# Re-ordering VectorE's and TensorE's lists in the first attention of a fused attention and GELU MLP

## The chip, the cores and the metric

The kernel runs on one core of one Trainium2 chip. Times are device microseconds (us) of one execution. Engines go by the names of the profile: PE is TensorE (PEld its weight loads), DVE is VectorE, ACT is ScalarE, POOL is GpSimd, and SP is the sync engine, which here only issues DMAs.

## The reference

Inputs are q, k and v of shape (8 batches, 12 heads, 448 positions, 64 wide), two gain rows g_q and g_k, and two weight matrices, 768 x 2048 and 2048 x 768. Attention runs on RMS-normed q and k; its output, with the heads side by side, goes through a two-layer MLP with the tanh form of GELU.

```python
q_n, k_n = (rmsnorm(q, g_q), rmsnorm(k, g_k))
scores = scale * np.matmul(q_n, k_n.transpose(0, 1, 3, 2))
attn = np.exp(scores - max);  attn = attn / (sum(attn) + 1e-09)
attn_out = np.matmul(attn, v)            # -> x, (3584, 768), heads side by side
h = x @ w_in
out = (0.5 * h * (1.0 + np.tanh(c * (h + 0.044715 * h * h * h)))) @ w_out
```

## The kernel before, in words

**Units.** A batch is cut into three chunks c = 0, 1, 2 of four heads. The 448 positions are cut into seven key tiles t = 0 to 6 of 64 positions. A *unit* (c, t) is four concurrent 64x64 matmuls (line 335) that make the scores of one key tile for four heads, 128 x 896 numbers, and one ACT exp of them (`ex`, line 339). A batch has 21 units; u0 to u20 below are those of batch 0, so u7 is the first of the middle chunk and u14 the first of the last chunk. The scores go to two PSUM buffers in turn (three from batch 1 on), so a unit's matmuls wait for the exp of the unit two before.

**What a chunk needs before its units.** Raw q and k arrive by DMA. Squares (line 161 on ACT, 163 on POOL) are summed on DVE (`total`, line 172). The inverse root of the mean comes from a log and an exp on ACT (`rsqrt`) in batch 0. For batch 1 DVE works it out with Newton steps: `rsqrt_newton` (lines 226 to 241) for chunks 0 and 2 and `rsqrt_last` (lines 253 to 263) for chunk 1. `normed` (line 275) multiplies; on DVE it reads the root from PSUM, on POOL from SBUF. `turn` (line 293) transposes the seven 128x128 pieces of a normed q or k on PE into a PSUM tile `tp`, and `put` (k: line 302, q: line 304 on ACT or 306 on DVE) copies that into `qT` or `kT`, k with the gains. Pieces 0 to 3 are called `t_first`, pieces 4 to 6 `t_rest`; `normed`, `turn` and `put` take either alone. A unit (c, t) needs all of its chunk's qT, but only piece t of kT.

**What comes after a chunk's units.** `products(..., 0)` sums the exps over the keys with matmuls against `ones` (line 386), `products(..., 1)` multiplies them with v. `turned` (395) transposes the sums on DVE, `recips` takes reciprocals of one column (401) and spreads them back with a second transpose of 128 x 896 (402), and `quad_x` (415) multiplies and writes xT, the MLP's input.

**PSUM.** The tag `mm` of the pool `ps_m` has two buffers that are handed out in turn. In batch 0 the takers are, in program order, the `tp` tiles, the tile `root` (inverse roots of chunk 2), and pairs of `os` tiles (`spared`, line 366), which hold the key sums of chunks 1 and 2. Each new taker waits until the tile two before it in that order has been read for the last time. `oall` holds the products, and also the roots of some chunks and the target `o` of `idle`.

**The order of the work.** It is written out by hand: each engine runs its list in program order. `first_attention` (582) loops over the 21 units of batch 0 and runs the entries of `mid` (lines 730 to 765) with the same number behind each. A slot below is such a number. Behind u20 come the remaining products, the last `quad_x`, and the first MLP layer of batch 0: `mm1_pair` (matmuls at 475, GELU at 480) and `mm1` (424, 430). In the loop over f, `m1` (784 to 792) places batch 1's sums, roots, norms and turns between these: `trans(1, c)` turns and puts q and k of a chunk; chunk 2 goes through DMA transposes instead (316). Then `attention(1, ...)` begins, with groups of units between the second layer's matmuls (445).

**At the start.** Sixteen `idle` matmuls (line 268) of a zero tile keep PE active while the first q and k arrive; pairs of them are placed in slots 0 to 4 and 9. DVE makes the zero tile with four memsets (81), and `ones` and `rows` with one each (634, 635).

Of the kernel before, what the change touches and what calls it, by code (L numbers as in the profile page):

```python
# [17 lines left out]
def kernel(  # L18
# [11 lines left out]
    nc = tc.nc  # L30
# [188 lines left out]
    def rsqrt_newton(b):  # L219


        rinvs[b] = smp.tile([P, NCH, 2, 2, NT], F32, tag="rinv", name="rinv")
        cs, flat = slice(0, NCH - 1), "p c n a t -> p (c n a t)"
        y, ms = rinvs[b][:, cs].rearrange(flat), sss[b][:, cs].rearrange(flat)
        t = smp.tile([P, NCH * 4 * NT], F32, tag="lg", name="lg")[:, :(NCH - 1) * 4 * NT]
        nc.vector.tensor_scalar(ms, ms, 1.0 / D, 1e-6, op0=ALU.mult, op1=ALU.add)
        nc.vector.tensor_scalar(
            y.bitcast(I32), ms.bitcast(I32), -0.5, float(0x5F3759DF), op0=ALU.mult, op1=ALU.add
        )
        for i in range(3):  # L230
            nc.vector.tensor_mul(t, y, y)
            nc.vector.scalar_tensor_tensor(t, t, -0.5, ms, op0=ALU.mult, op1=ALU.mult)
            if i < 2:
                nc.vector.scalar_tensor_tensor(y, t, 1.5, y, op0=ALU.add, op1=ALU.mult)
        m = 4 * NT
        for c in (1, 0):
            dst = y[:, c * m:(c + 1) * m] if c else place(b, c)
            nc.vector.scalar_tensor_tensor(  # L238
                dst, t[:, c * m:(c + 1) * m], 1.5, y[:, c * m:(c + 1) * m],
                op0=ALU.add, op1=ALU.mult,  # L240
            )

    def rsqrt_last(b):
# [44 lines left out]
    def turn(b, c, n, ts=slice(0, NT)):  # L288

        if ts.start == 0 and ts.stop == NT:  # L290
            tps[n] = ps_m.tile([128, 1024], BF16, tag="mm", name="tp")
        for t in range(ts.start, ts.stop):
            nc.tensor.transpose(  # L293
                tps[n][:, t * 128:(t + 1) * 128],
                nrms[n, b, c][:, t].rearrange("p a d -> p (a d)"), ident,
            )

    def put(b, c, n, ts=slice(0, NT), eng=nc.vector):
        dst = (kT if n == "k" else qT_of(b))[:, c, ts]
        src = tps[n][:, :TR].rearrange("p (t r s) -> p t r s", r=2, s=R)[:, ts]  # L300
        if n == "k":
            nc.vector.tensor_scalar(dst, src, gcol[:, 0:1], None, op0=ALU.mult)  # L302
        elif eng is nc.scalar:
            nc.scalar.copy(dst, src)
        else:
            nc.vector.tensor_copy(dst, src)
# [85 lines left out]
    def turned():  # L392
        st = oas["st"] = stp.tile([128, 2, S // 32, 32], F32, tag="st", name="st")
        for r in range(2):
            nc.vector.transpose(st[:, r].rearrange("p a b -> p (a b)"), oas[0][r])  # L395

    def recips():

        rb = oas["rb"] = stp.tile([128, 2, S], F32, tag="rb", name="rb")
        rc = smp.tile([128, 2 * S // 32], F32, tag="rc", name="rc")  # L400
        nc.vector.reciprocal(rc, oas["st"].rearrange("p r a b -> p (r a) b")[:, :, 0])
        nc.vector.transpose(  # L402
            rb.rearrange("p r s -> p (r s)"), rc.to_broadcast([128, 2 * S // 32, 32])
        )

    def quad_x(b, c):
        if c == 0:
# [251 lines left out]
    def warm():  # L659
        return oall[0][:, :S]  # L660
# [59 lines left out]
    for a in range(2):  # L720
# [5 lines left out]
    def turn_rest():  # L726
        tps["k"] = ps_m.tile([128, 1024], BF16, tag="mm", name="tp")
        turn(0, 0, "k", t_rest)

    mid = [(0, lambda: idle(2, warm())),  # L730
           (1, turn_rest, lambda: idle(2, warm())),
           (2, lambda: rsqrt(0, 1, near=(0, 1)), lambda: idle(2, warm())),
           (3, lambda: put(0, 0, "k", t_rest), lambda: normed(0, 1, "q", nc.vector),
            lambda: normed(0, 1, "k", nc.vector, t_first),
            lambda: normed(0, 1, "k", nc.vector, t_rest), lambda: idle(2, warm())),
           (4, lambda: idle(2, warm())),
           (5, lambda: turn(0, 1, "q"), lambda: put(0, 1, "q")),
           (6, lambda: turn(0, 1, "k"), lambda: put(0, 1, "k", t_first),
            lambda: put(0, 1, "k", t_rest)),
           (7, lambda: total(0, 2, "q"), lambda: total(0, 2, "k"),  # L740
            lambda: products(0, 0, 0, 0, 3)),
           (8, lambda: products(0, 0, 0, 3), lambda: turned(),
            lambda: rsqrt(0, 2, near=(1,)), lambda: normed(0, 2, "q", nc.gpsimd),
            lambda: normed(0, 2, "k", nc.vector, t_first),
            lambda: normed(0, 2, "k", nc.vector, t_rest), lambda: recips(),
            lambda: square(1, 0, "q", nc.gpsimd), lambda: w_in_part(1, 2),
            lambda: square(1, 0, "k", nc.gpsimd),
            lambda: w_out_part(0), lambda: load_v(1, 0, HP),
            lambda: square(1, 2, "q", nc.gpsimd), lambda: square(1, 2, "k", nc.gpsimd),
            lambda: w_out_part(1)),  # L750
           (9, lambda: idle(2, warm())),
           (10, lambda: products(0, 0, 1, 0, 3)),
           (11, lambda: products(0, 0, 1, 3)),
           (12, lambda: turn(0, 2, "q"), lambda: put(0, 2, "q"), lambda: turn(0, 2, "k"),
            lambda: put(0, 2, "k", t_first), lambda: put(0, 2, "k", t_rest),
            lambda: quad_x(0, 0)),

           (14, lambda: spared(), lambda: products(0, 1, 0, 0, 4)),
           (15, lambda: products(0, 1, 0, 4), lambda: turned(), lambda: recips()),
# [15 lines left out]
    def normed_both(b, c, eng):  # L775
        for n in "qk":
            normed(b, c, n, eng)

    m2 = []
    for b in range(B):  # L780
        m1, side, behind, ends = [], [], [], []
        if b == 0:

            m1 = [(0, lambda: total(1, 0, "k"),
                   lambda: total(1, 2, "q"), lambda: total(1, 2, "k"),
                   lambda: rsqrt_newton(1), lambda: normed_both(1, 2, nc.gpsimd)),
                  (2, lambda: total(1, 1, "q"), lambda: total(1, 1, "k"),
                   lambda: normed_both(1, 0, nc.vector), lambda: rsqrt_last(1),
                   lambda: normed_both(1, 1, nc.vector)),
                  (4, lambda: transposed(1, 2)),  # L790
                  (5, lambda: trans(1, 0)),
                  (7, lambda: trans(1, 1))]
            side += [(1, lambda: late_loads(2, 0)), (4, lambda: gain(1, 2)),
                     (2, lambda: late_loads(2, 1), lambda: late_loads(2, 2))]

            for n in "qk":
                sqs[n, 2, 1] = [
                    nrmp.tile([P, NT, 2, D], BF16, tag=f"nrm{m}", name="sq")
                    .rearrange("p t a d -> p (t a d)").bitcast(F32)
                    .rearrange("p (a t d) -> p a t d", a=1, t=NT) for m in "qk"  # L800
                ]
            for c, slots in ((0, (4, 4)), (1, (4, 4))):
                for n, slot in zip("qk", slots):
                    for hs in (slice(0, 1), slice(1, 2)) if c else (both,):
                        side.append(
                            (2, lambda c=c, n=n, hs=hs: square(2, c, n, nc.gpsimd, hs)))
                        behind.append((slot, lambda c=c, n=n, hs=hs: total(2, c, n, hs)))
        elif b + 1 < B:

            m1.append((0, lambda: gpsimd_waits(ess[b, NCH - 1][:1, 0, :1])))  # L810
            for c in range(NCH):
                if b == 1 and c + 1 == NCH:
                    m1 += [(0, lambda: total(2, 2, "q")), (0, lambda: total(2, 2, "k")),
                           (0, lambda: rsqrt_last(2))]
                m1 += [(0, lambda c=c: normed_both(b + 1, c, nc.gpsimd)),
                       (4 * c + 4, lambda c=c: transposed(b + 1, c))]
            m1 += [(9, lambda: gain(b + 1, 0)), (14, lambda: gain(b + 1, 1))]
# [73 lines left out]
```

## Time and profile before

| what | value |
|---|---|
| median of three runs | 405.93 us (405.3 to 406.69) |
| the profiled execution, its own time | 405.01 us |
| its span, first to last instruction | 403.2 us |
| granted TensorE clock | 1.000 |
| busy: PE / ACT / DVE / POOL | 393.8 / 280.1 / 259.8 / 121.3 us |
| PE busy from 52 us to 403 us (351 us) | 347.51 us |
| PE busy from 8 us to 30 us (22 us) | 19.07 us |
| first exp of batch 0 begins | 9.06 us |
| last exp of batch 0 ends | 29.65 us |
| first MLP matmul (line 475) begins | 30.41 us |
| first matmul of the second layer (line 445) begins | 51.70 us |

A busy time is a union over the engine's instructions; matmul ends are modelled, so a short wait of PE can be hidden in it. A timeline row gives start, length, engine, line, operation, tiles, shapes and count, and in brackets the idle time before it with what ended it. Neighbouring instructions on DVE and ACT overlap by some 0.08 to 0.1 us in the rows, so the distance from one start to the next is a little shorter than the length. The profiled execution took 0.92 us less than the median; the span is 1.8 us shorter than that execution's own time.

### The profile page before, as it was taken

What the parts mean: (1) busy time and instruction counts of PE and PEld (TensorE: products, weight loads), DVE (VectorE), ACT (ScalarE), POOL (GpSimd) and SP (SyncE); (2) the same over time, 40 slices, a digit from 0 to 9 for tenths busy, and PEclk for the clock granted to TensorE, in tenths of its full rate; (3) what the DMA queues carried; (4) which work ended last, traced back from release to release, by engine and by line L of the source; (5) the groups of instructions that cost most, each with busy time, mean ns of one, the idle gap of its engine ahead of it and who ended that gap; (6) DMA issues with size and microseconds to landing.
All of it is one profiled execution on the core that took longest, in us unless ns stands there. A gap on an engine that the chain in (4) does not pass through costs nothing.

```text
span 403.2 us, 8092 instructions
## 1 busy us (share of the span) xinstructions
PE 393.8 (98%) x3321; PEld 209.8 (52%) x3321; DVE 259.8 (64%) x438; ACT 280.1 (69%) x381; POOL 121.3 (30%) x101
## 2 busy tenths in 40 slices
PE   7899999999999999999999999999999999999996
PEld 3365555555555555554555555555555545555564
DVE  5989968975796369845699357963698405990010
ACT  6995398768974887847975789748878359744301
POOL 5992307454007230183004540072301800000000
PEclk9999999999999999999999999999999999999999
DMA  8999995898515954169612948149513511210033
GB/s 293 318 214 207 196 225 187 236 232 230 96 39 115 245 101 140 41 170 280 109 41 63 253 64 220 40 86 265 78 41 80 115 24 39 50 46 23 2 78 80
DMA packets 65561, 54.07 MB, mean 134 GB/s; under 512 B 37364, under 2 KB 60532, under 8 KB 65524
## 3 DMA queue, kind: packets, MB, share of 16 engines
q1 hardware_dynamic: 53184, 41.48, 39.0%
q0 software_dynamic: 12112, 11.80, 19.0%
q8 instruction: 26, 0.43, 0.4%
q10 hardware_dynamic: 228, 0.28, 0.2%
q14 instruction: 11, 0.09, 0.1%
HBM read 45.61 MB, written 11.01 MB: 140 GB/s over the span
## 4 chain that ended last, share of the span: by engine, by line
PE 89%; DVE 5%; ACT 2%; DMA 1%; issue 1%; POOL 0%; DVEq 0%
PE o L445 38%; PE h L424 24%; PE t L335 9%; PE t L386 8%; PE t L475 8%; ACT ex L339 2%; DVE ss L172 2%; PE o L386 1%; PE tp L293 1%; DMA rawq<-in_q_dram 1%; DVE nrmq L275 1%; DVE nrmk L275 0%; DVE st L395 0%; DVE xT L415 0%; DVE rb L402 0%
## 5 line engine op out<-in xcount | busy, mean ns | idle before, releaser
L339 ACT ACTIVATE ex<-t,shift 128x896 bf16<-128x896 f32 x168 | 157.6, 1005 | 22.7 <-PE t L335 20.1
L445 PE MATMUL o<-wout,g 128*128 128x384 bf16 (+1 forms) x912 | 156.8, 324 | 0.0
L445 PEld LDWEIGHTS <-g 128*128 128x128 bf16 x912 | 83.6, 98 | 67.8 <-issue 18.8
L424 PE MATMUL h<-xT,win 128*128 128x448 bf16 x516 | 99.1, 352 | 0.0
L172 DVE TENSOR_REDUCE ss<-sq 128x14 f32<-128x896 f32 (+3 forms) x45 | 44.3, 999 | 48.8 <-ACT sq L161 45.8
L424 PEld LDWEIGHTS <-win 128*128 128x128 bf16 x516 | 50.5, 98 | 47.1
L430 ACT ACTIVATE g<-h 128x448 bf16<-128x448 f32 x86 | 46.6, 543 | 28.2 <-PE h L424 23.1
L455 DVE COPY osb<-o 128x384 f32<-128x384 f32 x41 | 22.7, 554 | 52.4 <-PE o L445 50.7
L475 PE MATMUL t<-xT,win 128*128 128x448 bf16 x252 | 49.6, 352 | 0.0
L335 PE MATMUL t<-qT,kT 64*64 64x448 bf16 x672 | 47.1, 359 | 2.1 <-DVE kT L302 1.0
L480 ACT ACTIVATE g<-t 128x896 bf16<-128x896 f32 x21 | 18.4, 915 | 33.8 <-PE t L475 33.8
L664 POOL COPY mark<-es 1x1 bf16<-1x1 bf16 x6 | 1.1, 177 | 132.2 <-DVE es L357 132.2
L275 POOL TENSOR_TENSOR nrmq<-rawq,rinv 128x896 bf16<-128x896 f32 (+1 forms) x21 | 34.8, 1658 | 12.1 <-DVE o L238 7.6
L475 PEld LDWEIGHTS <-win 128*128 128x128 bf16 x252 | 24.5, 98 | 22.8 <-issue 0.6
L275 POOL TENSOR_TENSOR nrmk<-rawk,rinv 128x896 bf16<-128x896 f32 x19 | 31.9, 1679 | 0.0
L386 PE MATMUL t<-ex,vb 64*64 64x448 bf16 x588 | 31.6, 350 | 0.0
L335 PEld LDWEIGHTS <-kT 64*64 64x64 bf16 x672 | 17.3, 105 | 27.3 <-issue 20.9
L453 ACT COPY osb<-o 128x384 f32<-128x384 f32 (+1 forms) x16 | 7.3, 458 | 31.4 <-PE o L445 31.4
L163 POOL TENSOR_TENSOR sq<-rawq 128x896 f32<-128x896 f32 (+1 forms) x9 | 13.7, 1529 | 49.2 <-DVE ss L172 31.9
L402 DVE STREAM_TRANSPOSE rb<-rc 128x896 f32<-128x896 f32 x24 | 26.7, 1112 | 0.8
L360 DVE TENSOR_TENSOR e<-ex 128x896 bf16<-128x896 bf16 x33 | 20.0, 607 | 10.2 <-ACT ex L339 9.9
L386 PEld LDWEIGHTS <-vb 64*64 64x64 bf16 x672 | 20.3, 107 | 11.1 <-issue 2.4
(91 smaller groups left out, 307.2 us busy)
## 6 DMA issues: line engine op xcount, KB each, us to landing
out_dram<-osb SPq DMA_DIRECT2D x54, 192.0 KB, 2.7
rawq<-in_q_dram SPq DMA_DIRECT2D x23, 448.0 KB, 4.5
rawk<-in_k_dram SPq DMA_DIRECT2D x23, 448.0 KB, 5.3
vb<-in_v_dram POOLq DMA_DIRECT2D x7, 672.0 KB, 6.6
win<-in_moe_w_in_dram POOLq DMA_DIRECT2D x8, 384.0 KB, 10.8
wout<-in_moe_w_out_dram POOLq DMA_DIRECT2D x2, 1536.0 KB, 23.3
vb<-in_v_dram POOLq DMA_DIRECT2D x1, 448.0 KB, 7.9
qT<-nrmq SPq DMA_TRANSPOSE x19, 5.1
```

The source lines that it names most:

```text
L172: nc.vector.reduce_sum(sss[b][:, seat(b, c), "qk".index(n), hs, ts], squares(b, c, n, hs, ts), axis=AX.X)
L275: eng.tensor_mul(nrms[n, b, c][:, ts].rearrange("p t a d -> p a t d"), raws[n, b, c][:, :, ts], root[:, :, ts].to_broadcast([P, 2, m, D]),)
L335: nc.tensor.matmul(sc[r * R:(r + 1) * R, a, :S], kT[rs, c, t, r], qT[b][rs, c, :, r], start=True, stop=True,)
L339: nc.scalar.activation(ex[:, t], sc[:, :, :S], AF.Exp, scale=scale, bias=shift)
L360: nc.vector.tensor_add(e2, ex[:, t - 1], ex[:, t])
L386: nc.tensor.matmul(o[r][a * D:(a + 1) * D], vb[b % 2][rs, 2 * c + a, i] if what else ones[rs], es[i][rs, a], start=(i == 0), stop=(i == n ...
L402: nc.vector.transpose(rb.rearrange("p r s -> p (r s)"), rc.to_broadcast([128, 2 * S // 32, 32]))
L424: nc.tensor.matmul(h[:, :S], win[:, c, f * 128:(f + 1) * 128], xT[b][:, c], start=(c == 0), stop=(c == HP - 1),)
L430: nc.scalar.activation(g[:, f, (b % 2) * S:(b % 2 + 1) * S], h[:, :S], AF.Gelu_apprx_tanh)
L445: nc.tensor.matmul(o, g[:, f, i * 128:(i + 1) * 128], wout[:, f, lo:hi], start=(f == 0), stop=(f == nf - 1),)
L455: nc.vector.tensor_copy(osb[:, lo:hi], o)
L475: nc.tensor.matmul(h[:, j, :S], win[:, c, f * 128:(f + 1) * 128], xT[b][:, c], start=(c == 0), stop=(c == HP - 1),)
```

## The change

1. *Idle matmuls.* The zero tile and its four memsets go. `idle` reads a constant 1.0 instead, one element repeated. The memset of `ones` becomes three and that of `rows` two.
2. *Newton root of batch 1.* The last step writes only q's half of chunk 0 (14 columns) to PSUM and the other 42 columns to SBUF.
3. *Chunk 0 of batch 1.* `normed(1, 0, "k")` moves from DVE to POOL, behind POOL's two norms of chunk 2. `trans(1, 0)` moves from behind f = 5 to behind f = 6, and q's copy in it from DVE to ACT.
4. *First attention, chunk 1.* At slot 5, q is turned and put, and then only the first four pieces of k. The norm of k's other three pieces moves from slot 3 to slot 8 (ahead of `turned`), their turn and put from slot 6 to slot 9. The `total`s of chunk 2 move from slot 7 to 6.
5. *First attention, chunk 2.* The norm of k moves from slot 8 to 9. k is turned at slot 11 instead of 12, ahead of q, and its first four pieces are put there. q is turned and put at 12. The put of k's other pieces moves from slot 12 to 13, behind `quad_x(0, 0)`.
6. *Reciprocals of chunk 0.* `recips` is split: `recip` at slot 9 and two halves `spread` at 11 and 12. `products(0, 0, 1)` is cut again behind its fifth tile, with the rest and `quad_x(0, 0)` at slot 13.

```diff
-    zeros = consts.tile([128, S], BF16)
-    for i in range(4):
-        nc.vector.memset(zeros[:, i * S // 4:(i + 1) * S // 4], 0.0)
+    filler = nc.const_aps.tensor(1.0, [128, S], BF16)
...
-        m = 4 * NT
-        for c in (1, 0):
-            dst = y[:, c * m:(c + 1) * m] if c else place(b, c)
+        m = 2 * NT
+        for js, dst in ((slice(m, None), y[:, m:]), (slice(0, m), place(b, 0)[:, :m])):
...
-            nc.tensor.matmul(w, zeros[:, :128], zeros, start=True, stop=True)
+            nc.tensor.matmul(w, filler[:, :128], filler, start=True, stop=True)
...
-    def trans(b, c):
+    def trans(b, c, eng=nc.vector):
         for n in "qk":
             turn(b, c, n)
-            put(b, c, n)
+            put(b, c, n, eng=eng)
...
+    def recip():
+        oas["rb"] = stp.tile([128, 2, S], F32, tag="rb", name="rb")
+        rc = oas["rc"] = smp.tile([128, 2 * S // 32], F32, tag="rc", name="rc")
+        nc.vector.reciprocal(rc, oas["st"].rearrange("p r a b -> p (r a) b")[:, :, 0])
+    def spread(rs=slice(0, 2)):
+        m = S // 32
+        rc = oas["rc"][:, rs.start * m:rs.stop * m]
+        nc.vector.transpose(
+            oas["rb"][:, rs].rearrange("p r s -> p (r s)"),
+            rc.to_broadcast([128, (rs.stop - rs.start) * m, 32]),
+        )
     def recips():
+        recip()
+        spread()
...
-    nc.vector.memset(ones, 1.0)
-    nc.vector.memset(rows, (D ** 0.5) * (1 + 2.0 ** -7))
+    for i in range(3):
+        nc.vector.memset(ones[:, i * D // 4:(i + 1 + i // 2) * D // 4], 1.0)
+    for i in range(2):
+        nc.vector.memset(rows[:, i * P // 2:(i + 1) * P // 2], (D ** 0.5) * (1 + 2.0 ** -7))
...
-            lambda: normed(0, 1, "k", nc.vector, t_first),
-            lambda: normed(0, 1, "k", nc.vector, t_rest), lambda: idle(2, warm())),
+            lambda: normed(0, 1, "k", nc.vector, t_first), lambda: idle(2, warm())),
            (4, lambda: idle(2, warm())),
-           (5, lambda: turn(0, 1, "q"), lambda: put(0, 1, "q")),
-           (6, lambda: turn(0, 1, "k"), lambda: put(0, 1, "k", t_first),
-            lambda: put(0, 1, "k", t_rest)),
-           (7, lambda: total(0, 2, "q"), lambda: total(0, 2, "k"),
-            lambda: products(0, 0, 0, 0, 3)),
-           (8, lambda: products(0, 0, 0, 3), lambda: turned(),
+           (5, lambda: turn(0, 1, "q"), lambda: put(0, 1, "q"),
+            lambda: turn_new(1, t_first), lambda: put(0, 1, "k", t_first)),
+           (6, lambda: total(0, 2, "q"), lambda: total(0, 2, "k")),
+           (7, lambda: products(0, 0, 0, 0, 3)),
+           (8, lambda: products(0, 0, 0, 3), lambda: normed(0, 1, "k", nc.vector, t_rest),
+            lambda: turned(),
             lambda: rsqrt(0, 2, near=(1,)), lambda: normed(0, 2, "q", nc.gpsimd),
-            lambda: normed(0, 2, "k", nc.vector, t_first),
-            lambda: normed(0, 2, "k", nc.vector, t_rest), lambda: recips(),
...
-           (9, lambda: idle(2, warm())),
+           (9, lambda: turn(0, 1, "k", t_rest), lambda: put(0, 1, "k", t_rest),
+            lambda: normed(0, 2, "k", nc.vector, t_first),
+            lambda: normed(0, 2, "k", nc.vector, t_rest), lambda: recip(),
+            lambda: idle(2, warm())),
            (10, lambda: products(0, 0, 1, 0, 3)),
-           (11, lambda: products(0, 0, 1, 3)),
-           (12, lambda: turn(0, 2, "q"), lambda: put(0, 2, "q"), lambda: turn(0, 2, "k"),
-            lambda: put(0, 2, "k", t_first), lambda: put(0, 2, "k", t_rest),
-            lambda: quad_x(0, 0)),
+           (11, lambda: products(0, 0, 1, 3, 5), lambda: turn(0, 2, "k"),
+            lambda: put(0, 2, "k", t_first), lambda: spread(slice(0, 1))),
+           (12, lambda: turn(0, 2, "q"), lambda: put(0, 2, "q"),
+            lambda: spread(slice(1, 2))),
+           (13, lambda: products(0, 0, 1, 5), lambda: quad_x(0, 0),
+            lambda: put(0, 2, "k", t_rest)),
            (14, lambda: spared(), lambda: products(0, 1, 0, 0, 4)),
...
-                   lambda: rsqrt_newton(1), lambda: normed_both(1, 2, nc.gpsimd)),
+                   lambda: rsqrt_newton(1), lambda: normed_both(1, 2, nc.gpsimd),
+                   lambda: normed(1, 0, "k", nc.gpsimd)),
                   (2, lambda: total(1, 1, "q"), lambda: total(1, 1, "k"),
-                   lambda: normed_both(1, 0, nc.vector), lambda: rsqrt_last(1),
+                   lambda: normed(1, 0, "q", nc.vector), lambda: rsqrt_last(1),
                    lambda: normed_both(1, 1, nc.vector)),
                   (4, lambda: transposed(1, 2)),
-                  (5, lambda: trans(1, 0)),
+                  (6, lambda: trans(1, 0, nc.scalar)),
                   (7, lambda: trans(1, 1))]
```

More of the change, by code (lines that the diff above doesn't have):

```diff
@@ L234, in rsqrt_newton @@
                 nc.vector.scalar_tensor_tensor(y, t, 1.5, y, op0=ALU.add, op1=ALU.mult)
-        m = 4 * NT
-        for c in (1, 0):
-            dst = y[:, c * m:(c + 1) * m] if c else place(b, c)
+        m = 2 * NT
+        for js, dst in ((slice(m, None), y[:, m:]), (slice(0, m), place(b, 0)[:, :m])):
             nc.vector.scalar_tensor_tensor(
-                dst, t[:, c * m:(c + 1) * m], 1.5, y[:, c * m:(c + 1) * m],
-                op0=ALU.add, op1=ALU.mult,
+                dst, t[:, js], 1.5, y[:, js], op0=ALU.add, op1=ALU.mult
             )
@@ L395, in turned @@
             nc.vector.transpose(st[:, r].rearrange("p a b -> p (a b)"), oas[0][r])
-    def recips():
[L399 to L404, printed above, removed]
+    def recip():
[9 more added lines that the diff above has]
+        )
+    def recips():
+        recip()
+        spread()
     def quad_x(b, c):
```

6 lines of the change are left out of this document (3 added, 3 removed).

## The prediction

> **What bounds the kernel now.** I read the busy time by stage first. From 52 us on PE is busy 347.51 of 351 us, and the list of what PE waited for has no entry there: whatever moves the first matmul of the second layer (51.70 us) moves the end by the same amount. So only the time before 52 us counts. There ACT's timeline comes next: in the first attention it runs exps back to back.
>
> ```profile
> 9.06 2.80 ACT L339 ACTIVATE ex<-t,shift 128x896 bf16<-128x896 f32 x3
> 12.23 3.68 ACT L339 ACTIVATE ex<-t,shift 128x896 bf16<-128x896 f32 x4
> 16.06 1.90 ACT L339 ACTIVATE ex<-t,shift 128x896 bf16<-128x896 f32 x2
> 17.92 0.32 ACT L197 ACTIVATE lg<-ss,eps 128x28 f32<-128x28 f32 x1
> 18.49 11.16 ACT L339 ACTIVATE ex<-t,shift 128x896 bf16<-128x896 f32 x12
> ```
>
> Three exps in 2.80 us at 1.00 each are 0.90 from start to start. Four from 12.23 would let u7 begin at 15.80; it begins at 16.06, so 0.26 us are lost. Twelve from 18.49 should last 10.9 and last 11.16; the chain of waits puts an exp at 22.30, behind a unit matmul that ended at 22.28, so about 0.2 is lost there, at u13. The rest of this stretch is exps and the small root rows. Then PE and DVE in the same stretch:
>
> ```profile
> 15.62 0.38 PE L335 MATMUL t<-qT,kT 64*64 64x448 bf16 x4 [0.58 <-DVE kT L302]
> 21.38 0.55 PE L293 MATMUL tp<-ident,nrmk 128*128 128x128 bf16 x7
> 21.86 0.38 PE L335 MATMUL t<-qT,kT 64*64 64x448 bf16 x4
> 22.65 0.38 PE L335 MATMUL t<-qT,kT 64*64 64x448 bf16 x4 [0.40 <-DVE kT L302]
> 22.86 1.06 PE L386 MATMUL os<-ex,ones 64*64 64x448 bf16 x16
> 22.12 0.80 DVE L302 TENSOR_SCALAR kT<-tp,gcols 128x512 bf16<-128x512 bf16 x2
> 22.84 1.15 DVE L415 TENSOR_TENSOR xT<-o,rb 128x448 bf16<-128x448 f32 x2
> 24.59 1.18 DVE L395 STREAM_TRANSPOSE st<-os 128x448 f32<-128x448 f32 x2 [0.60 <-PE os L386]
> ```
>
> u7 waits for the put of k (15.62). u13 (21.86) stands behind fourteen transposes. The `os` matmuls (22.86) start as the puts of q and k, which empty the two `mm` buffers, end at 22.2 and 22.9. Last, the end of the first MLP layer:
>
> ```profile
> 49.26 0.62 DVE L306 COPY qT<-tp 128x896 bf16<-128x896 bf16 x1
> 49.69 0.92 ACT L480 ACTIVATE g<-t 128x896 bf16<-128x896 f32 x1 [1.35 <-PE t L475]
> 49.93 0.55 PE L293 MATMUL tp<-ident,nrmq 128*128 128x128 bf16 x7 [0.28 <-DVE qT L306]
> 50.52 0.55 PE L293 MATMUL tp<-ident,nrmk 128*128 128x128 bf16 x7
> 51.01 0.76 PE L335 MATMUL t<-qT,kT 64*64 64x448 bf16 x12
> 51.70 3.42 PE L445 MATMUL o<-wout,g 128*128 128x384 bf16 x20
> ```
>
> PE waits for copies of chunk 0 that DVE reaches only at 49.26, because DVE is busy without a pause from 33.31 (the chain of waits runs through it).
>
> **Part A, idle matmuls and memsets.** Four memsets go (0.30 us in all) and three come, each no longer than the 0.17 of `rows`. DVE has nothing to do until 4.59; without that cover it would be about 0.2 us. The sixteen idle matmuls begin at 1.18, behind the zero tile, whose first memset begins at 0.82; they can begin about 0.33 sooner. The start is set by the landing of raw q at 3.96, so nothing is gained. Whether a repeated element streams as fast no row shows; even at twice 0.19 us the pairs in slots 0 to 4 stand in PE's idle time before the next unit: 0 taken, 0.1 at most, at slot 9.
>
> **Part B, chunk 1.** DVE from 13.33: k's first norm ends at about 14.0 (0.57 to the next start), the other 0.46 are gone from here. q's transposes end at 14.15, so q's put runs from 14.19 instead of 14.39; k's first put follows 0.54 later and lasts 0.48, to 15.21 instead of 15.57. PE starts u7 at 15.27, its scores are there at 15.65, and the exp can begin at 15.80, its place. **Gain 0.26**, with 0.1 to spare. The totals follow at 15.12 and end at 17.2; the log at slot 8 is ready behind u8, and u9 begins at 18.23 instead of 18.49. At slot 8 k's other norm (0.46) stands before `turned`, which still starts at 17.57 (before: 17.80). PE's idle pair waits for it until 18.29, so u10 loses some 0.06. SP: the load into the raw k buffer of chunk 1 (issued at 14.54) now waits for the later norm, to 17.6. Nothing stands behind it on SP before 41.98, and its data are first squared on ACT at 38.64; it landed at 24.40, so over 10 us cover the delay. POOL's list starts with the root at 18.59, now some 0.26 sooner.
>
> **Part C, chunk 2.** With k turned a unit sooner, u13 is behind seven transposes instead of fourteen: **gain about 0.2**. But DVE's list gets longer ahead of the put of k's last pieces. From start to start: totals 15.12 + 1.98 = 17.10; norm 0.46, `turned` 1.09, put 0.33: 18.98; two norms 1.04 and the reciprocal 0.35: 20.37; wait for k's transposes, which need the norm that ends at 20.1, about 0.25: 20.62; put 0.39, half spread 0.56 (half of 1.11), put of q 0.54, half spread with its end 0.66: 22.77; `quad_x` 1.06: 23.83; put of k's rest 0.41: **24.24**. Before, that put ended at 22.92, ahead of `quad_x`.
>
> Who waits for it? The order of the two `mm` buffers was q, k, os, os. It becomes k, q, os, os, so the *first* `os` tile takes k's buffer, and its first matmul, at slot 14, waits for the put behind `quad_x`. Behind it on PE stands u15. So the `os` matmuls start at about 24.29 instead of 22.87: 1.42 later. u15's exp: 24.29 + 0.76 (four rounds of four matmuls at 0.19) + 0.37 + 0.05 = 25.47, where 23.7 was its place. From here both chains carry the delay. ACT: five more exps at 0.90, u20 begins at 29.95 instead of 28.6. DVE: `turned` of chunk 1 follows the `os` matmuls, at 24.59 + 1.42, and PE's products at 28.47, which wait for `quad_x(0, 1)`, move by the same 1.42. PE had only 0.52 of idle time left between 22.65 and 30.4. So the MLP begins **1.4 us later**, at 31.8, and the 0.26 and 0.2 above are lost again. Bounds: nothing lost and 0.46 gained, if the put were over by 22.5; 1.8 if DVE meets one more wait of 0.4, the longest it had here before (0.35 at 12.33). I take 1.4, from the rows of the very instructions.
>
> **Part D, the MLP stretch** (in the clock of before). DVE loses one norm (0.99 from start to start) and one copy (0.54), so chunk 1's norms end at 48.3 instead of 49.3. POOL gets a norm of 1.68 (its rows of that shape) behind 43.61, where it has nothing else: ends at 45.3. PE runs the sixth pair before the turns of chunk 0, which then come at 46.4 (q) and 46.8 (k): both norms are there. ACT copies q at about 47.5: between 0.48 (three of the seven pieces at the start took that) and 1.01 (an exp of this shape); I take 0.9; it lies in the 1.35 that ACT idles before the GELU at 49.69. k's put ends at 48.95. So at 49.49, when the last pair's matmuls are issued, both `tp` buffers are free: fourteen transposes of 0.056 to 50.27, three units of 0.19 to 50.84, the first second-layer matmul at 50.95 instead of 51.70. **Gain 0.75.** What is late next: ACT's first exp stays at 51.92 (GELU, then table load), and u5 of batch 1, now at 54.68, waits for the exp that ends at 54.72: 0.09 lost. Net 0.66. Bounds: 0, if ACT or POOL takes the place of DVE, and 0.75. The split of the Newton step keeps two instructions of about 0.2: nothing.
>
> **Sum.** +1.40 - 0.66 = +0.74 us. The profiled execution would go from 405.01 to 405.75, its span from 403.2 to 403.9. It lies 0.92 below the median; taking the difference to the median gives 405.93 + 0.74 = **406.7**.
>
> **The rivals.**
> *(1) The `os` wait does not come.* Its place is slot 14, its price the whole 1.4, and it decides at 22.5: if k's rest is put by then, u15 is in time. Then 0.45 is gained in the first attention and 0.66 after: 405.93 - 1.1 = 404.8, faster. For it: DVE starts the totals 0.7 sooner. Against: the sum of DVE's rows is 1.7 too long, and the `os` matmuls' dependence on these puts is visible before.
> *(2) The MLP stretch gains nothing*, because POOL's norm or ACT's copy is late. POOL would have to be 1.5 late, ACT 1.1. Then 405.93 + 1.4 = 407.3.
> *(3) PE's clock falls at the start.* Weight loads of the idle matmuls stand 0.37 apart until 4.12 and PE then works twice as fast; this took 2.94 us of activity. The idle matmuls now end 0.33 sooner, so the stretch to the next one (8.01), with little but transposes in it, grows from 2.33 to 2.66 us. Before, 2.33 did not hurt: two idle matmuls from 8.94 on took 0.55 together. If 2.66 does, four transposes cost 0.22 more, u0 0.19 and the next three units 0.24 each (1.13 of PE work at half speed against 0.89 of ACT): 1.1 in all, and 407.8. [...]
>
> **How the numbers follow.** Forecast 0.62, rival 1 0.14, rival 2 0.11, rival 3 0.05, others (more waits in DVE's longer list, mostly upward) 0.08. About 0.3%, 1.2 us, is what a measurement of this kernel tells from no change; the three runs differ by 1.4. Faster by that means under 404.7: nearly half of rival 1 and a little more, 0.08. Slower means over 407.15: most of rival 2, nearly all of rival 3, a twelfth of the forecast, half of the others, 0.21. The same: 0.71. The range 404.9 to 407.7 leaves out about half of rivals 1 and 3 and the far ends, under 0.2; the forecast's own is 406.2 to 407.2.
>
> **What would show it.** Right: u7 at 15.8, u9 at about 18.2, then one gap of about 1.7 us on ACT before u15; PE's first `os` matmul at about 24.3, released by the put at line 302, which follows `quad_x`; the first MLP matmul at about 31.8; no wait of PE for DVE before the turns of chunk 1 in batch 1; the first second-layer matmul at about 52.4. Wrong: exps without a gap from u9 to u20 (rival 1); a wait at the last turns (rival 2); idle matmuls 0.37 apart behind 8 us (rival 3).

## The result

The changed kernel takes 408.62 us (median of 20 runs, 407.19 to 412.23) against 406.09 us for the kernel before in the same runs. The ratio is 1.0063, 95% interval 1.0042 to 1.0085, or 1.7 to 3.5 us: slower. The prediction was +0.74 us and "the same", with a range that ended at 407.7 us.

The profiled execution of the changed kernel took 407.21 us, its span is 405.4 us, 2.2 longer than before. The table cuts both spans at the same events: the start of the exp u3, of the first MLP matmul, and of the first matmul of the second layer.

| stretch, us | before | after | difference | forecast |
|---|---|---|---|---|
| start to u3 | 12.23 | 12.34 | +0.11 | 0 |
| u3 to the first MLP matmul | 18.18 | 19.59 | +1.41 | +1.40 |
| from there to the second layer | 21.29 | 21.57 | +0.28 | -0.75 |
| second layer to the end | 351.52 | 351.93 | +0.41 | +0.09 |

So the first attention lost what was forecast, the MLP stretch lost instead of gaining, and 0.41 was lost behind 52 us, where 0.09 was forecast. ACT's timeline after shows the first of these, one gap of 1.55 us ahead of u15:

```profile
12.34 5.48 ACT L336 ACTIVATE ex<-t,shift 128x896 bf16<-128x896 f32 x6
17.68 0.35 ACT L195 ACTIVATE lg<-ss,eps 128x28 f32<-128x28 f32 x1
...
18.28 5.86 ACT L336 ACTIVATE ex<-t,shift 128x896 bf16<-128x896 f32 x6
25.68 5.50 ACT L336 ACTIVATE ex<-t,shift 128x896 bf16<-128x896 f32 x6 [1.55 <-PE t L332]
```

PE and DVE at the same place, from their timelines after:

```profile
20.40 0.56 PE L290 MATMUL tp<-ident,nrmk 128*128 128x128 bf16 x7
20.89 0.38 PE L332 MATMUL t<-qT,kT 64*64 64x448 bf16 x4
...
22.82 0.35 PE L383 MATMUL os<-ex,ones 64*64 64x448 bf16 x2
24.51 0.94 PE L383 MATMUL os<-ex,ones 64*64 64x448 bf16 x14 [1.34 <-DVE kT L299]
...
23.02 1.11 DVE L421 TENSOR_TENSOR xT<-o,rb 128x448 bf16<-128x448 f32 x2
24.06 0.40 DVE L299 TENSOR_SCALAR kT<-tp,gcols 128x384 bf16<-128x384 bf16 x1
```

The put of k's rest (line 299, 24.06) stands behind the two multiplies of `quad_x`, and fourteen of the sixteen `os` matmuls wait for it until 24.51. The first two, into the other buffer, had run at 22.82.

The end of the MLP stretch, DVE and POOL in their timelines after:

```profile
43.08 3.33 POOL L272 TENSOR_TENSOR nrmk<-rawk,rinv 128x896 bf16<-128x896 f32 x2
...
43.26 1.08 DVE L272 TENSOR_TENSOR nrmq<-rawq,o 128x896 bf16<-128x896 f32 x1
44.26 0.54 DVE L250 TENSOR_SCALAR ss<-ss 128x28 f32<-128x28 f32 x1
44.84 1.61 DVE L251 TENSOR_SCALAR rinv<-ss 128x28 int32<-128x28 int32 x1
46.48 0.19 DVE L255 COPY o<-rinv 128x28 f32<-128x28 f32 x1
...
51.20 0.68 DVE L299 TENSOR_SCALAR kT<-tp,gcols 128x896 bf16<-128x896 bf16 x1
...
51.93 0.55 PE L290 MATMUL tp<-ident,nrmq 128*128 128x128 bf16 x7 [0.89 <-DVE kT L299]
```

Two instructions on 28 columns take 0.54 and 1.61 us; the same two took 0.17 and 0.18 before, when POOL had ended its one norm of k at 43.61:

```profile
41.93 1.68 POOL L275 TENSOR_TENSOR nrmk<-rawk,rinv 128x896 bf16<-128x896 f32 x1
...
44.12 0.17 DVE L253 TENSOR_SCALAR ss<-ss 128x28 f32<-128x28 f32 x1
44.33 0.18 DVE L254 TENSOR_SCALAR rinv<-ss 128x28 int32<-128x28 int32 x1
```

After, POOL's two norms of k run from 43.08 to 46.41, and the second of the slow instructions ends at 46.45. DVE's chain is 1.8 us longer for it, and PE waits 0.89 at the last turns.

The list of PE's waits after, from 52 us on, has one entry besides those last turns (waiting instruction, what it waited for, us in total, times, longest):

```profile
PE t L383 <- DVE es L354: 0.4, 1, 0.4
```

The timelines show that sum of keys on DVE at 1.94 instead of 0.62 us, under a square on POOL:

```profile
61.65 1.94 DVE L354 TENSOR_TENSOR es<-es,ex 128x896 bf16<-128x896 bf16 x1
...
61.43 1.68 POOL L161 TENSOR_TENSOR sq<-rawq 128x896 f32<-128x896 f32 x1 [15.03 <-DMA rawq<-in_q_dram]
```

Before, the add was over when the square began, and they did not meet:

```profile
59.85 0.62 DVE L357 TENSOR_TENSOR es<-es,ex 128x896 bf16<-128x896 bf16 x1
...
60.92 1.68 POOL L163 TENSOR_TENSOR sq<-rawq 128x896 f32<-128x896 f32 x1 [17.31 <-DMA rawq<-in_q_dram]
```

### The profile page after: what moved, and what is told of

Its sections match the earlier page's. It is cut to its first block, busy times and chain, and to the rows that moved or that the text cites. A ratio compares the mean times of both kernels' runs of the same rounds, so it can differ in the third digit from the quotient of the medians.

```text
span 405.4 us, 8096 instructions
## 1 busy us (share of the span) xinstructions
PE 394.6 (97%) x3321; PEld 208.9 (52%) x3321; DVE 260.9 (64%) x436; ACT 281.4 (69%) x382; POOL 123.4 (30%) x102
## 4 chain that ended last, share of the span: by engine, by line
PE 87%; DVE 7%; ACT 1%; DMA 1%; POOL 1%; issue 1%; SPq 0%; DVEq 0%
PE o L451 37%; PE h L430 24%; PE t L332 9%; PE t L383 8%; PE t L481 8%; DVE ss L170 2%; DMA rawq<-in_q_dram 1%; ACT ex L336 1%; POOL g L161 1%; DVE rb L403 1%; DVE nrmq L272 1%; PE tp L290 0%; PE o L383 0%; DVE es L354 0%; DVE xT L421 0%
## 5 line engine op out<-in xcount | busy, mean ns | idle before, releaser
L272 POOL TENSOR_TENSOR nrmk<-rawk,rinv 128x896 bf16<-128x896 f32 x20 | 33.6, 1680 | 0.0
L403 DVE STREAM_TRANSPOSE rb<-rc 128x896 f32<-128x896 f32 (+1 forms) x25 | 26.8, 1073 | 0.8
```

Source lines behind the costliest of these rows:

```text
L272: eng.tensor_mul(nrms[n, b, c][:, ts].rearrange("p t a d -> p a t d"), raws[n, b, c][:, :, ts], root[:, :, ts].to_broadcast([P, 2, m, D]),)
L403: nc.vector.transpose(oas["rb"][:, rs].rearrange("p r s -> p (r s)"), rc.to_broadcast([128, (rs.stop - rs.start) * m, 32]),)
```

## The experiments

The theory: three losses with separate causes. (a) The `os` wait. (b) POOL's added norm, beside which two tensor_scalars of DVE take 0.54 and 1.61 us instead of 0.17 and 0.18. (c) The same once more at the sum of keys (1.94 instead of 0.62), because everything is late. The expectations call (b) and (c) the port; no trace shows a port, and the word stands for the longer times alone. Its rivals: another wait takes the place of (a); the slow instructions of (b) are a pause of VectorE that has moved there (program loading in the expectations, a guess), since DVE's idle time of 0.5 us ahead of the last `quad_x`, which the profile before has, is gone in the profile after.

Two runs of the same kernel differ at the start. The load of chunk 1's raw q landed between 6.72 and 9.61 us in these profiles, and from about 7.6 on u3 came later with it. So I compare stretches, and give the ratio of the timed runs beside them.

| kernel | q lands | u3 | u3 to MLP | MLP stretch | to the end | ratio (95%) |
|---|---|---|---|---|---|---|
| before | 6.72 | 12.23 | 18.18 | 21.29 | 351.52 | 1 |
| before, again | 7.40 | 12.35 | 18.18 | 21.31 | 351.43 | 0.9987 (0.9951 to 1.0022) |
| after | 7.63 | 12.34 | 19.59 | 21.57 | 351.93 | 1.0063 (1.0042 to 1.0085) |
| e1, put first | 8.79 | 13.49 | 18.03 | 21.55 | 351.42 | 1.0003 (0.998 to 1.0027) |
| e2, norm on DVE | 8.73 | 13.43 | 19.59 | 20.77 | 351.89 | 1.001 (0.9981 to 1.004) |
| e3, guess in PSUM | 9.12 | 13.82 | 19.59 | 20.52 | 351.50 | 1.0017 (0.9991 to 1.0043) |
| e4, both | 7.38 | 12.53 | 18.02 | 20.52 | 351.59 | 0.9968 (0.9942 to 0.9993) |
| e5, constant only | 7.11 | 12.18 | 18.18 | 20.89 | 351.74 | 0.9974 (0.9943 to 1.0005) |
| e6, first attention only | 9.61 | 14.31 | 20.64 | 20.90 | 351.95 | 1.0042 (1.001 to 1.0075) |
| e7, MLP stretch only | 9.46 | 14.42 | 18.18 | 21.56 | 351.44 | 1.0003 (0.9969 to 1.0037) |
| e9, three memsets | 7.32 | 12.51 | 18.18 | 20.89 | 351.52 | 0.997 (0.995 to 0.9989) |
| e10, constant and a memset | 8.90 | 13.60 | 18.18 | 21.31 | 351.41 | 0.9981 (0.9963 to 0.9998) |
| e11, best | 7.35 | 12.05 | 17.86 | 20.52 | 352.03 | 0.9961 (0.9946 to 0.9976) |
| e12, double norm | 7.49 | 12.21 | 18.18 | 22.42 | 351.43 | 1.0028 (1.0 to 1.0055) |

**e1: the put ahead of `quad_x`.**

```diff
-           (12, ..., lambda: put(0, 2, "q"), lambda: spread(slice(1, 2))),
-           (13, lambda: products(0, 0, 1, 5), lambda: quad_x(0, 0), lambda: put(0, 2, "k", t_rest)),
+           (12, ..., lambda: put(0, 2, "q"), lambda: put(0, 2, "k", t_rest), lambda: spread(slice(1, 2))),
+           (13, lambda: products(0, 0, 1, 5), lambda: quad_x(0, 0)),
```

> The changed kernel, with the put of k's last three pieces of chunk 2 moved from behind quad_x(0, 0) to slot 12, right behind the put of q. Theory: three losses, each with its own cause: the os wait (about 1.5 us), the two slow tensor_scalars of rsqrt_last (1.8 us of VectorE), and one slow add of key sums in batch 1 (1.3 us of VectorE, 0.4 us of TensorE), which only meets POOL's square because everything is late. Then the os wait goes, the first MLP matmul comes at about 30.0 us instead of 31.93, the two tensor_scalars stay at 0.5 and 1.6 us, TensorE still waits at the last turns, the first second-layer matmul comes at about 51.6 us, the slow add is gone, and the span is about 403.2 us: the ratio to before is 0.999 to 1.001. Rival: the os wait was only the visible one of a chain, and another wait in VectorE's list takes its place; then the MLP still begins after 31 us.

The stretch falls from 19.59 to 18.03, so all of (a) goes with one put moved: 1.56 us. From PE's timeline of e1, the `os` matmuls now follow their unit at once:

```profile
23.76 0.38 PE L332 MATMUL t<-qT,kT 64*64 64x448 bf16 x4
23.97 1.05 PE L383 MATMUL os<-ex,ones 64*64 64x448 bf16 x16
24.73 0.48 PE L332 MATMUL t<-qT,kT 64*64 64x448 bf16 x4
```

The slow sum of keys is gone too (351.42), which it should be if only the lateness made it meet POOL. The first MLP matmul still comes after 31 us (31.51), the sign that I had given to the rival, but only because u3 came 1.15 us later than in the profile after, with q's load; no other long wait stands in the stretch. Against before, 0.15 us are gained in it and not the 0.45 that I expected. From u3 to u9 it takes 5.94 instead of 6.26 us, but from u9 to u13 3.96 instead of 3.81: the stall of 0.21 ahead of u13 has gone, and two have come that the profile after has too. Ahead of u10 0.21 is lost, as a pair of idle matmuls waits for `turned`, which now stands behind k's other norm, and ahead of u12 0.14, as k's seven transposes stand in front of that unit. PE after:

```profile
17.93 0.34 PE L290 MATMUL tp<-ident,nrmk 128*128 128x128 bf16 x3 [0.48 <-DVE nrmk L272]
18.48 0.54 PE L265 MATMUL o<-const-bfloat16-1.0 128*128 128x448 bf16 x2 [0.21 <-DVE st L392]
```

**e2: the norm of k back on DVE.**

```diff
-        m = 2 * NT
+        m = 4 * NT
...
-                   lambda: rsqrt_newton(1), lambda: normed_both(1, 2, nc.gpsimd),
-                   lambda: normed(1, 0, "k", nc.gpsimd)),
+                   lambda: rsqrt_newton(1), lambda: normed_both(1, 2, nc.gpsimd)),
...
-                   lambda: normed(1, 0, "q", nc.vector), lambda: rsqrt_last(1),
+                   lambda: normed_both(1, 0, nc.vector), lambda: rsqrt_last(1),
```

> The changed kernel, with the norm of k of chunk 0 of batch 1 back on VectorE (and its root back in PSUM). Theory of the port: POOL's norms and VectorE's tensor_scalars from SBUF to SBUF exclude each other, so without POOL's third norm both tensor_scalars take 0.2 us again (they come after 44.9 us, when POOL has just ended its second norm). VectorE saves 1.8 and pays 1.0 for the norm: the last turns wait some 0.25 us instead of 1.2, the first second-layer matmul is at about 52.7 us instead of 53.50, the slow add of key sums may go too (0.4), the span is 404.2 to 404.7 us, ratio 1.002 to 1.004. Rival, a pause in loading VectorE's program that has moved to this place (before, VectorE had a pause of 0.5 us ahead of the last quad_x that the changed kernel doesn't show): a tensor_scalar near there stays long, and the time gets longer by the norm's 1.0 us rather than shorter.

From DVE's timeline of e2:

```profile
45.34 1.08 DVE L272 TENSOR_TENSOR nrmk<-rawk,o 128x896 bf16<-128x896 f32 x1
46.34 0.17 DVE L250 TENSOR_SCALAR ss<-ss 128x28 f32<-128x28 f32 x1
46.55 0.18 DVE L251 TENSOR_SCALAR rinv<-ss 128x28 int32<-128x28 int32 x1
```

Both take 0.2 us again, and the stretch is 0.80 us *shorter* with one norm more on DVE. The theory of (b) said 0.8; the rival said longer. The slow sum of keys stayed here.

**e3: POOL's norm kept, `rsqrt_last` without tensor_scalars from SBUF to SBUF.**

```diff
-        nc.vector.tensor_scalar(ms, ms, 1.0 / D, 1e-6, op0=ALU.mult, op1=ALU.add)
         nc.vector.tensor_scalar(
-            y.bitcast(I32), ms.bitcast(I32), -0.5, float(0x5F3759DF), op0=ALU.mult, op1=ALU.add
+            z.bitcast(I32), ms.bitcast(I32), -0.5, float(0x5F3759DF + (3 << 23)), op0=ALU.mult, op1=ALU.add
         )
+        nc.vector.tensor_copy(y, z)
         for i in range(3):
-            nc.vector.tensor_copy(z, y)
+            if i:
+                nc.vector.tensor_copy(z, y)
             nc.vector.tensor_mul(t, z, y)
-            nc.vector.scalar_tensor_tensor(t, t, -0.5, ms, op0=ALU.mult, op1=ALU.mult)
+            nc.vector.scalar_tensor_tensor(t, t, -0.5 / D, ms, op0=ALU.mult, op1=ALU.mult)
```

> The changed kernel with POOL's norm kept, but without any tensor_scalar from SBUF to SBUF in rsqrt_last: the first guess of the Newton step is written to PSUM and copied from there, and the scaling of the mean is folded into the constants (the 1e-6 beside the mean square is left out there, and one instruction fewer runs). Theory of the port: no long instruction there, VectorE's chain ends over 2 us sooner, TensorE waits for nothing at the last turns, the first second-layer matmul is at about 52.4 us, the span about 404.0 us, ratio 1.001 to 1.003. Rival, a pause of program loading: an instruction near there still takes over 1 us.

From the timelines of e3, POOL and DVE; `o` lies in PSUM, `ss` and `rinv` in SBUF:

```profile
44.56 3.33 POOL L274 TENSOR_TENSOR nrmk<-rawk,rinv 128x896 bf16<-128x896 f32 x2
...
45.74 0.18 DVE L250 TENSOR_SCALAR o<-ss 128x28 int32<-128x28 int32 x1
45.95 0.18 DVE L254 COPY rinv<-o 128x28 f32<-128x28 f32 x1
46.17 0.20 DVE L258 TENSOR_TENSOR o<-o,rinv 128x28 f32<-128x28 f32 x1
```

POOL runs the same two norms at the same point, and the tensor_scalar that writes to PSUM takes 0.18 beside them. The stretch is 20.52, 1.05 less than after. No instruction of `rsqrt_last` takes over 0.20 us, where the rival had one of over 1 us.

**e4: both edits.**

> The two edits of the runs before together: the put ahead of quad_x and rsqrt_last without tensor_scalars from SBUF to SBUF (again without the 1e-6 there). Theory: the first attention then has neither the old stalls nor the new one, the MLP begins at about 30.0 us, no wait at the last turns, the first second-layer matmul at about 50.6 us, the span about 402.1 us, ratio about 0.997: faster than both kernels. Rival: what is gained in the first attention is lost again at some other wait, and the ratio stays at 1.000.

18.02 and 20.52: the two effects add up, and the kernel beats both (0.9968, 0.9942 to 0.9993).

**The parts alone.** "Before, again" is the kernel before without an edit. e5 takes the constant and the split memsets from the diff and nothing else, e6 that and the first attention (the diff's parts 1 and 4 to 6), e7 that and the MLP stretch (its parts 1 to 3).

> The kernel before, unchanged, profiled once more. In the profiles of the runs above the first loads of chunk 1's raw q landed at 7.4 to 9.1 us, in the first profile of the kernel before at 6.72, and the exp u3 came 0.1 to 1.5 us later with them. If that is chance of the DMA queues, this profile can land anywhere between 6.7 and 9 and the time is the same within 0.2%; if it comes with the constant for the idle matmuls, this profile lands near 6.7 again. Behind u3 the stretches are those of the first profile: 18.2 us to the first MLP matmul, 21.3 from there to the second layer.

> The kernel before with only the constant for the idle matmuls and the split memsets. Theory: nothing waits for it; the idle matmuls begin about 0.4 us sooner, and the stretches behind u3 are those of before (18.2 and 21.3 us), ratio 0.998 to 1.002. Rival: the constant makes the first loads land later, for whatever reason: raw q of chunk 1 lands after 7.4 us, u3 is 0.5 to 1.5 us later than in the second profile of the kernel before, ratio 1.001 to 1.004.

> The kernel before with the constant and the new order of the first attention, without the changes to the MLP stretch (norm of k on VectorE, turns of chunk 0 behind f = 5, copy of q on VectorE). Theory: the os wait alone: from u3 to the first MLP matmul 19.6 us instead of 18.2, from there to the second layer 21.3 as before, since VectorE's chain is shifted with TensorE; perhaps 0.4 at the slow add of key sums. Ratio 1.003 to 1.005. Rival: part of the 1.4 us is caught up in the MLP stretch, which then is under 21.0 us.

> The kernel before with the constant and the changes to the MLP stretch (norm of k on POOL, turns of chunk 0 behind f = 6, q's copy on ACT), with the first attention in its old order. Theory of the port: from u3 to the first MLP matmul 18.2 us; the two tensor_scalars take 0.5 and 1.6 us again, and the MLP stretch is 21.6 us instead of 21.3; ratio 1.000 to 1.002. Rival: POOL's norms and those two only met because the first attention was late; then both take 0.2 us here, the stretch is 20.5 to 20.7 us and the ratio 0.998.

e7 has the two slow tensor_scalars (0.54 and 1.61) with the first attention in its old order, so (b) is the MLP part's own. In e6, u13 to u20 take 7.91 us as in the profile after (6.31 before), so (a) is the first attention's own; its 20.64 holds 1.05 more, lost before u13, behind the latest loads of all: PE's granted clock was 0.50 there from 15.7 to 19.1 us, and u6 came 1.48 us behind u5 instead of 0.89. Against e5's rival, q landed at 7.11 there. But e5 and e6 contradict me in one point: their MLP stretch is 20.9, not 21.3. Either the constant or the count of DVE's instructions had taken 0.4 us away. In DVE's timeline before, the idle time of 0.51 ahead of the last `quad_x` is put down to DVE's own transpose, which had ended 0.50 us before:

```profile
33.31 1.16 DVE L415 TENSOR_TENSOR xT<-o,rb 128x448 bf16<-128x448 f32 x2 [0.51 <-DVE rb L402]
```

That multiply is the 64th record of DVE in the trace, waits for semaphores counted; the only other such pause, 0.47 us at 106.45 before a sum of keys, is ahead of the 192nd, 128 further. In e7 one of 0.46 us stands at 211.44, again before a sum of keys, and that is the 320th: 128 further still. Two experiments tell the count from the constant.

**e9 and e10: the count of instructions.** e9 is the kernel before with three memsets for its zero tile, e10 is e5 with one memset more.

```diff
-    for i in range(4):
-        nc.vector.memset(zeros[:, i * S // 4:(i + 1) * S // 4], 0.0)
+    for i in range(3):
+        nc.vector.memset(zeros[:, i * S // 3:(i + 1) * S // 3], 0.0)
```

> The kernel before with the zero tile made by three memsets instead of four, and nothing else. Theory of program loading: VectorE pauses some 0.4 us ahead of its 64th and 192nd instruction, unless that one follows an instruction that still runs. With one instruction fewer, the 64th is the second multiply of the last quad_x, right behind the first, and the pause is hidden: the idle time ahead of that quad_x falls from 0.5 to 0.1 us and the stretch from the first MLP matmul to the second layer from 21.3 to 20.9 us, as with the constant for the idle matmuls; ratio 0.998 to 1.000. Rival: it was the constant itself that took the 0.4 us away; then this kernel has 21.3.

> The kernel before with the constant for the idle matmuls and the split memsets, and one small memset more on VectorE at the start (eps is written twice), so that VectorE has as many instructions ahead of the last quad_x as before. Theory of program loading: the pause of 0.5 us is back ahead of quad_x and the MLP stretch takes 21.3 us instead of 20.9. Rival, the constant itself: 20.9 us stay.

DVE's timeline of e9:

```profile
31.97 1.11 DVE L402 STREAM_TRANSPOSE rb<-rc 128x896 f32<-128x896 f32 x1
33.19 1.15 DVE L415 TENSOR_TENSOR xT<-o,rb 128x448 bf16<-128x448 f32 x2
```

and of e10:

```profile
33.07 1.11 DVE L400 STREAM_TRANSPOSE rb<-rc 128x896 f32<-128x896 f32 x1
34.70 1.15 DVE L413 TENSOR_TENSOR xT<-o,rb 128x448 bf16<-128x448 f32 x2 [0.52 <-DVE rb L400]
```

One memset fewer at the start takes the pause away 30 us later (20.89), one more brings it back (21.31). The constant has no part in it. What VectorE does in the pause is not shown. Program loading was my guess from the distance of 128 records; in the trace of before no transfer of instructions runs during the pause (32.81 to 33.31 us), the nearest begin at 27.11 and 34.42.

**e12: the disputed cost by itself.** The kernel before, with POOL doing its norm of chunk 2's k twice.

```diff
-                   lambda: rsqrt_newton(1), lambda: normed_both(1, 2, nc.gpsimd)),
+                   lambda: rsqrt_newton(1), lambda: normed_both(1, 2, nc.gpsimd),
+                   lambda: normed(1, 2, "k", nc.gpsimd)),
```

> The kernel before, with POOL's norm of k of chunk 2 of batch 1 done twice, and nothing else; nothing needs the second sooner than some 10 us later. It keeps POOL busy to 45.3 us instead of 43.6, while VectorE runs rsqrt_last from 44.1. Theory of the port: the first tensor_scalar of rsqrt_last, begun at about 44.1, takes until POOL ends, 1.2 us instead of 0.2; the rest of the chain, sums and products that touch PSUM, keeps its durations; the last turns wait 1.0 us more, and the MLP stretch takes 22.3 to 22.5 us instead of 21.3. Rival: POOL costs VectorE nothing, and the stretch stays at 21.3.

From the timelines of e12:

```profile
41.91 3.45 POOL L275 TENSOR_TENSOR nrmk<-rawk,rinv 128x896 bf16<-128x896 f32 x2
...
43.10 1.08 DVE L275 TENSOR_TENSOR nrmk<-rawk,o 128x896 bf16<-128x896 f32 x1
44.10 1.30 DVE L253 TENSOR_SCALAR ss<-ss 128x28 f32<-128x28 f32 x1
45.43 0.18 DVE L254 TENSOR_SCALAR rinv<-ss 128x28 int32<-128x28 int32 x1
```

A norm that nobody on DVE waits for costs 1.13 us of this stretch, and 0.3% of the timed runs (0 to 0.55%): the tensor_scalar ends at 45.40, as POOL does (41.91 + 3.45 = 45.36). The norm at 43.10, with one input in PSUM, keeps its 1.08 beside POOL.

**e11: k of chunk 2 in two turns.** e4, also without the 1e-6 in `rsqrt_last`, with this edit:

```diff
-           (11, ..., lambda: turn(0, 2, "k"), ...
-           (12, lambda: turn(0, 2, "q"), lambda: put(0, 2, "q"), lambda: put(0, 2, "k", t_rest), ...
+           (11, ..., lambda: turn_new(2, t_first), ...
+           (12, lambda: turn(0, 2, "q"), lambda: put(0, 2, "q"), lambda: turn(0, 2, "k", t_rest),
+            lambda: put(0, 2, "k", t_rest), ...
```

> The kernel with the put ahead of quad_x and rsqrt_last without tensor_scalars from SBUF to SBUF (without the 1e-6 there), and k of chunk 2 turned in two steps: its first four pieces at slot 11, the other three at slot 12 behind q. Theory: what is left of the first attention's stalls, 0.35 us ahead of u12, stems from PE's wait for the norm of k's last pieces; with the two steps u9 to u13 take 3.6 us instead of 3.96, u3 to the first MLP matmul 17.7 instead of 18.0, the MLP stretch stays at 20.5, ratio 0.995 to 0.997. Rival: the stall moves to u13 or u14, since q's transposes and the rest of k's now stand together behind u12, and 18.0 stays.

It is the best measured, 404.38 us (0.9961, 0.9946 to 0.9976), but it does not tell itself apart from e4 by that. The stretch is 17.86, 0.16 less than e4's, where I expected 0.3. The stall ahead of u12 is gone and 0.06 shows at u13, so the rival is half right; but the larger part of the 0.35 had never been there: the 0.21 ahead of u10 stays. And behind 52 us it gives 0.4 back, in a longer meeting with POOL: the gain of k (line 321), 1.00 us in e4, takes 1.42, and PE waits 0.3 for the multiply behind it. DVE's timeline of e11:

```profile
63.10 1.42 DVE L321 TENSOR_SCALAR kT<-kT,gcols 128x896 bf16<-128x896 bf16 x1
```

## Why the prediction was wrong, step by step

**Part A (0 forecast): a gain of 0.4 missed.** The count of DVE's instructions ahead of the last `quad_x` changes the place of the pause, and the sum had no term for it. In the kernel after, the 64th record is the transpose that spreads the reciprocals, the pause doesn't show, and the MLP stretch would be 20.9 without the rest (e5, e6). The idle matmuls began at 0.78, 0.40 sooner where 0.33 was forecast, but did not end sooner: they took 5.11 us instead of 4.66, as they stood 0.37 apart until 4.47 instead of 4.12. That time is not set by the edit: "before, again", the same kernel as before, has it at 6.36. So the premise of rival 3, a longer pause behind them, did not come about in the profile after.

The lower clock that rival 3 feared did come in two others. In e7 PE never waited longer than 1.14 us between 6.6 and 9.6, but had little except transposes to do; its granted clock then was 0.50 for 3.4 us, from 9.62, and u1 and u2 came 1.39 and 1.70 us behind the unit before them instead of 0.9. In e6 it was 0.50 from 15.73 on, soon after a wait of 1.50 us. What brings it on is not shown; the 0.05 of rival 3 was an estimate.

**Part B (+0.26 gained): right.** u3 to u7 took 3.56 instead of 3.83.

**Part C (1.4 lost): right in size, +1.41, and in cause.** e1 shows the cause with one put moved. Two details were off. The tile that waits is the second `os` tile, not the first, so the two buffers do not simply alternate as I had read it; one put still decides, since PE runs its list in order: u15's matmuls, behind the `os` matmuls of 24.51, began at 25.11. And the 0.2 gained at u13 was outweighed by 0.21 lost at u10, where 0.06 was forecast, and 0.14 at u12, while the put ended at 24.46 instead of 24.24; u15 began at 25.68, forecast 25.47.

**Part D (0.66 gained): wrong, 0.28 lost.** This is the step that failed: "so chunk 1's norms end at 48.3 instead of 49.3". POOL's norm was priced by asking whether POOL would be done in time. It was, at 46.41, well ahead of PE. What was not asked is what DVE would be doing meanwhile. Two tensor_scalars from SBUF to SBUF stood there, and took 1.8 us more. With neither of them going from SBUF to SBUF (e3) the stretch is 0.77 shorter than before, close to the 0.75 forecast, and the missing term was worth 1.05 of it (21.57 to 20.52). Of those 0.77 e5 has 0.40 without part D, from the vanished pause. But in e3 chunk 1's norms end at 50.75 and PE turns them at 52.36, so my estimate is that the pause's 0.4 would have been covered there: part D and the missing pause remove the same wait of PE, and the arithmetic of what PE can save held. The measured +0.28 hides part of the loss: counted from e5's 20.89, part D alone cost 0.68. Rival 2 had the outcome, nothing gained, and its sign, a wait at the last turns, by a mechanism that did not occur (POOL or ACT late).

The profile before had the evidence. This row of DVE's timeline, a tensor_scalar in SBUF that takes 0.44 to 0.45 when POOL is idle, takes 1.00 beside POOL's square at 64.20:

```profile
64.38 1.00 DVE L322 TENSOR_SCALAR kT<-kT,gcols 128x896 bf16<-128x896 bf16 x1
```

The profiles show when such an instruction is slow: beside POOL, 0.18 becomes 1.61 and ends 0.04 us behind it (after); an add of two SBUF tiles, 0.62, becomes 1.94 (after); a tensor_scalar that writes PSUM stays at 0.18 (e3); a norm that reads its root from PSUM stays at 1.08 (e12); and the sums take 2.07 for two beside POOL's norms and without them (before, 40.14 and 35.38). Over the fourteen profiles, all 7 of the Newton roots' tensor_scalars from SBUF to SBUF and all 3 adds of key sums that begin in the middle of a tensor_tensor of POOL are slow, and of the other 65 and 1663 none is. A tensor_scalar of one column (`shift`, 0.15 at 8.67, under POOL's square from 7.46 to 9.14) was not slow. The row at 64.38 spoke against this change, and the prediction did not weigh it.

**The end moves with the first second-layer matmul: nearly.** That matmul came 1.80 later (53.50 against 51.70), the end 2.2. POOL's squares start when a load lands, so they do not shift with PE (60.92 became 61.43, while the add moved from 59.85 to 61.65), and the delay pushed a sum of keys into one of them (0.4).

**The chances.** 0.71 for "the same" rested on two terms of opposite sign, of which only one had been checked against what the other engines run at that time.

## What to carry to other kernels

Moving an elementwise operation to GpSimd was not free for VectorE here (1.8 us in two tensor_scalars, 1.3 in an add): list what VectorE runs during that time, and give a tensor_scalar or an add between SBUF operands another place, or try one operand in PSUM (0.18 in e3). When a copy that empties a PSUM buffer moves down a list (1.56 us here), look who gets the buffer next, and what stands behind that one in its engine's queue. Compare kernels that differ by 0.3% by stretches between the same events, not by spans.

## What the runs showed of the hardware

- VectorE paused some 0.4 to 0.5 us ahead of its 64th and 192nd record, in e7 ahead of its 320th, and it only showed where the record ahead was a wait for a semaphore, not running work. The distance was 128 records. One memset more or less at the start is worth 0.4 us of the MLP stretch here (21.31 in e10, 20.89 in e9).
- How long PE's first matmuls stood 0.37 us apart before they came every 0.19 differed between executions: until 4.12 and 6.36 us in two profiles of the kernel before, from 3.75 (e12) to all sixteen (e3, the last at 6.33) over the fourteen.
- PE's granted clock fell to 0.50 for 3.4 us in e6 and e7, without a wait of PE longer than 1.50 us ahead of it.
- The landing of the same early load varied by 2.9 us between executions (6.72 to 9.61), the exp u3 by 2.4. Why was not tried. All six landings later than 8.7 came in the ten kernels with the constant, none in the four without it; e5, timed as a whole, is not slower for it (0.9974), so whether the constant has a part in them stays open.
